# Second-half softmax split in two pieces, its sums and weights placed in the third group of weighting steps; inverse pieces and loads placed anew

## The chip, the cores and the metric

The kernel runs on one NeuronCore of a Trainium2 chip. The time is device microseconds of one execution, from start to end on that core; lower is better. Five engines work side by side, each through its own list of instructions in order: TensorE (PE in the profile, its weight loads PEld), VectorE (DVE), ScalarE (ACT), GpSimd (POOL) and SyncE (SP). SP and POOL also issue the transfers (DMA) of this part of the kernel. An engine waits at an instruction until the semaphores it needs are up, and everything behind that instruction in its list waits too.

## The reference

Two independent operators share one launch; the outputs stand side by side in the last axis. S = L = 2048 positions, D = 640.

```python
# A: 32 heads of 20; each position looks at W=8 positions back, 2 apart
qkv = (x @ wqkv)...                       # q, k, v: [32 heads, 2048, 20]
logits = einsum("bhsd,bhswd->bhsw", q, kg) * 20**-0.5    # kg[s,w] = k[s - 2w]
attn = softmax(where(mask, logits, -1e9))                # over the 8 offsets w
o = einsum("bhsw,bhswd->bhsd", attn, vg)                 # vg[s,w] = v[s - 2w]
a = o.reshape(S, D) @ wo
# B: a diagonal state space kernel K[640, 2048], and the causal convolution with it
K = einsum("dn,dnl,dn->dl", Cc, exp(logdA * l), dB).real
y = irfft(rfft(pad(K)) * rfft(pad(u)))[:2048] + u * Dskip
return concatenate([a, y], axis=-1)
```

## The kernel before

Part B comes first and runs until about 340 us: tables of exponentials and sines, the kernel K by matmuls, and Fourier transforms as matmuls, one chunk c of 128 channels after the other (five chunks). Of its inverse transform the first half ends in DRAM (`Zdram`), and the product of u and the skip factor in `UDdram`. Part A's projections and logits run between and after it. The change is in the last stage, from about 352 us, where three kinds of work share the engines.

**Weighting steps.** `av_step(i0, ni, j0, nj, w)` handles one of the eight offsets w for ni positions of each of four sequence quarters and nj of the five blocks of four head channels. VectorE multiplies v, shifted by 2w, with the weight `at[:, w]` (line 585, tile `prod` or `atp`: a ring of six buffers, two of which are parts of the tile `atp`), then sixteen 32x32 matmuls with the identity add the product into two accumulators `ps_o` of TensorE. After w = 7 ScalarE writes both accumulators to `o` (line 595). So a step's product can't be written before TensorE has read the one six steps earlier. There are six groups of eight steps. By the numbers that the code gives (first position, positions, first block, blocks): the first is (0, 256, 0, 2), then (0, 128, 2, 3), (128, 128, 2, 3), (256, 128, 0, 4), (256, 256, 4, 1) and (384, 128, 0, 4). The first three belong to the first half of the positions (`at[0]`), the last three to the second half (`at[1]`). Three `ps_o` accumulators exist, two of which a group holds, so the second matmul half of a new group waits until ScalarE has emptied the old group's first accumulator.

**Output projection.** `out_proj(q)` makes eight pieces for positions quarter q, each of five 128x128 matmuls with 320 columns (`ps_op<-wo,o`), one evacuation (line 611 on ScalarE, or 609 on VectorE for half of the last eight) and for every second piece a write to the output. The list `rest` holds these pieces. Quarter 0 needs `o` of the first two groups, quarter 1 the third, quarter 2 the fourth and fifth, quarter 3 the sixth.

**Second half of the inverse transform.** 24 pieces in the list `parts` (three for each eight rows, of 3, 3 and 2 rows), each of 12 or 8 matmuls (`ps_ib<-Z,HB`) and one evacuation (line 653) to `ysb`; after each third piece four writes to the output (line 656, on SP). Six pieces use one of four loads `Z` (line 640: fifteen transfers of 128 KB, five chunks of three). The loads 0 and 1 are issued at once; of the loads 2 and 3 single chunks are issued between weighting steps (`LOADS`). Loads 1 and 2 go through SP alone, 0 and 3 through SP and POOL. Pieces of `rest` and `parts` share the two one-bank accumulators.

**Softmax.** `softmax_a(hf)` takes the maximum over the eight offsets (a tree of three operations, line 542), subtracts it, and ScalarE takes the exponential (line 548). `softmax_b(hf)` adds up (a tree of three, line 552), takes the reciprocal (line 557) and writes the weights `at[hf]` (line 561).

From `att.in_order()` on, the matmuls stand in TensorE's list in the order in which the Python code issues them (all recorded at line 420). Instructions of the other engines are put in an order by the planner, unless `keep_in_program_order` holds them. Before the change the planner set VectorE's order: it put weighting step 0 ahead of the last two products of the logits (line 521), and the five operations of `softmax_b(1)` between weighting steps of the first and second group. The code that places it all:

```python
    for w in range(W):                                   # first group
        if w < 2:   fill(parts, 3 - w)
        elif w > 4: fill(parts)
        ...
        att.av_step(0, 256, 0, 2, w)
        if w == 2:   att.softmax_a(1)
        elif w == 4: att.softmax_b(1)
```

In the other five groups a step is followed by a piece of `parts` (second group, odd w; fifth group, each w), by a piece of `rest` (third, fourth and sixth group, each w), and in the sixth group at even w by a piece of `parts` as well.

Of the kernel before, what the change touches and what calls it, by code (L numbers as in the profile page):

```python
# [402 lines left out]
class Attention:  # L403
# [146 lines left out]
    def softmax_b(self, hf):  # L550
        nc, lsb = self.nc, self.lsb[hf]
        TT = lambda o, a, b, op: nc.vector.tensor_tensor(out=o, in0=a, in1=b, op=op)
        tr = self.ta.tile([128, 4, 256], f32, name="tree", tag="TA0")
        TT(tr[:], lsb[:, 0:4], lsb[:, 4:8], A.add)
        TT(tr[:, 0:2], tr[:, 0:2], tr[:, 2:4], A.add)
        TT(tr[:, 0], tr[:, 0], tr[:, 1], A.add)
        nc.vector.reciprocal(out=tr[:, 1], in_=tr[:, 0])
        if hf == 0:
            self.AP_ = self.ta.tile([128, 4, 2048], bf16, name="atp", tag="R1")
        self.at[hf] = self.AP_[:, hf].rearrange("p (w i) -> p w i", w=W)  # L560
        TT(self.at[hf], lsb, tr[:, 1].unsqueeze(1).to_broadcast([128, W, 256]), A.mult)

    def open_out(self, a2):
        nc = self.nc
        self.o = a2.tile([128, 5, S], bf16, name="o")
        self.o4 = self.o[:].rearrange("p j (s i) -> p j s i", s=4)
        self.wo = self.ta.tile([128, 5, D], bf16, name="wo", tag="TX")
        wsrc = self.A_wo.rearrange("(h j dd) e -> dd h j e", j=5, dd=4)
        for dd in range(4):
            nc.gpsimd.dma_start(out=self.wo[32 * dd:32 * dd + 32], in_=wsrc[dd])  # L570
        self.ob = self.ta.tile([128, 6, D], bf16, name="ob", tag="cT")
        ring = self.ta.tile([128, 4, 2048], bf16, name="prod2", tag="R0")
        self.ring = [self.AP_[:, 2], self.AP_[:, 3]] + [ring[:, i] for i in range(4)]

    def av_step(self, i0, ni, j0, nj, w):

        nc = self.nc
        MM = self.MM
        at, n = self.at[i0 // 256], nj * ni
        if w == 0:  # L580
            self.ops = [self.big("ps_o") for _ in range(2)]
        p2 = self.ring[self.nav % 6][:, 0:4 * n]
        self.nav += 1
        off = HALO + i0 - DIL * w
        nc.vector.tensor_tensor(out=p2.rearrange("p (d i) -> p d i", i=ni), in0=self.v2[:, 4 * j0:4 * j0 + 4 * nj, off:off + ni],  # L585
                                in1=at[:, w, i0 % 256:i0 % 256 + ni].unsqueeze(1).to_broadcast([128, 4 * nj, ni]), op=A.mult)
        p2v = p2.rearrange("p (j dd i) -> p dd j i", dd=4, i=ni)
        for sc in range(4):
            for dd in range(4):
                sl = slice(32 * sc, 32 * sc + 32)  # L590
                MM(self.ops[sc // 2][32 * dd:32 * dd + 32, sc % 2, 0:n].rearrange("p (j i) -> p j i", i=ni), lhsT=self.ident[sl, sl], rhs=p2v[sl, dd],
                   start=(w == 0), stop=(w == W - 1), tile_position=(32 * sc, 32 * dd), skip_group_check=True)
        if w == W - 1:
            for f, p in enumerate(self.ops):
                nc.scalar.copy(out=self.o4[:, j0:j0 + nj, 2 * f:2 * f + 2, i0:i0 + ni], in_=p[:, :, 0:n].rearrange("p s (j i) -> p j s i", i=ni))  # L595
# [66 lines left out]
def body(tc, ctx, pools, prm, B_u, B_Dskip, Sd, Zd, UDd, A_x, A_wqkv, A_wo, out_a, out_b):  # L662
    nc = tc.nc
# [33 lines left out]
    att = Attention(tc, pools, A_x, A_wqkv, A_wo, out_a, psk, psg)  # L697
# [86 lines left out]
    a2 = ctx.enter_context(tc.tile_pool(name="a2", bufs=1, side="right", reuse_waits="tile"))  # L784
# [20 lines left out]
    parts = inv.parts()  # L805
    rest = []

    def fill(some, n=1):
        for f in some[0:n]:
            f()  # L810
        del some[0:n]

    for w in range(W):
        if w < 2:
            fill(parts, 3 - w)
        elif w > 4:
            fill(parts)
        if w == 0:
            att.open_out(a2)
        att.av_step(0, 256, 0, 2, w)  # L820
        if w == 2:
            att.softmax_a(1)
        elif w == 4:
            att.softmax_b(1)
    LOADS = {(d, w + 2 * (qr == 3)): (qr, c) for c, (d, w) in enumerate(((0, 0), (0, 4), (1, 0), (1, 4), (None, 0))) for qr in (2, 3)}
    for i0, ni, j0, nj, done in ((0, 128, 2, 3, 0), (128, 128, 2, 3, 1), (256, 128, 0, 4, None), (256, 256, 4, 1, 2), (384, 128, 0, 4, 3)):
        for w in range(W):
            att.av_step(i0, ni, j0, nj, w)
            if (done, w) in LOADS:
                qr, c = LOADS[done, w]  # L830
                inv.load(qr, c, c + 1)
            if done == 2 or done == 0 and w % 2 == 1:
                fill(parts)
            elif done == 0:
                pass
            else:
                fill(rest)
                if done == 3 and w % 2 == 0:
                    fill(parts)
        if done is not None:  # L840
            rest += att.out_proj(done, done == 3)
    for f in parts + rest:
# [4 lines left out]
def kernel(  # L847
# [61 lines left out]
```

## Time and profile before

| | before |
|---|---|
| median of three runs | 439.84 us (439.48 to 441.04) |
| the profiled execution, its own time | 438.98 us |
| span of its trace, first to last instruction | 437.2 us |
| VectorE busy over the span | 391.3 us (89%) |
| TensorE busy over the span | 358.4 us (82%) |
| ScalarE busy over the span | 314.0 us (72%) |
| mean granted TensorE clock | 0.916 |

The profile comes from one execution. Engines' busy times overlap, so shares of the span add up to more than one. A timeline row gives start, duration, engine, line, operation, tiles (written <- read), shapes and how many instructions are merged in the row; in square brackets stands how long the engine sat idle before, and what ended the wait. Durations of neighbouring instructions of one engine overlap a little, so what a piece costs in a dense stretch is the distance from start to start. A row of the windows view gives, for a stretch of time, the busy time (and instructions) of each engine, then the granted clock as a share of full speed, the busy share of the DMA engines and GB/s.

### The profile page before, as it was taken

The numbers are of one execution on the slowest core, as the hardware profiler recorded it, in microseconds if no ns is written. First come the engines' busy times: TensorE is split into PE (matmuls) and PEld (weight loads), VectorE is DVE, ScalarE is ACT, GpSimd is POOL, SyncE is SP. The second block draws the span as 40 slices with busy tenths as digits, with TensorE's granted clock in tenths as the row PEclk, the third lists the DMA queues.
The fourth block names the chain that finished last, engine by engine and source line by source line (L and its number), as shares of the span: only waits on it lengthen the run. The fifth ranks groups of instructions, "written<-read, shape, count | busy, mean of one in ns | idle before, by whom it ended". The sixth has DMA issues, their size and how long they took to land.

```text
span 437.2 us, 17687 instructions
## 1 busy us (share of the span) xinstructions
PE 358.4 (82%) x8041; PEld 241.1 (55%) x8041; DVE 391.3 (89%) x386; ACT 314.0 (72%) x570; POOL 44.5 (10%) x85
## 2 busy tenths in 40 slices
PE   1397659989886998879778799999899897399995
PEld 0145546866863677556665665545555674134443
DVE  7889999999997999999999989946978989999751
ACT  3974998889999899979997845342858344544663
POOL 7440000000000000000010000400001204102110
PEclk9996577999999898889999899999999999659999
DMA  5569102163233402324079933500210907957343
GB/s 143 186 141 200 18 3 109 39 227 94 99 123 123 97 28 98 144 103 99 27 258 241 236 75 135 178 0 3 67 32 1 265 17 201 228 141 225 96 107 114
DMA packets 45131, 51.62 MB, mean 118 GB/s; under 512 B 31376, under 2 KB 38992, under 8 KB 42368
## 3 DMA queue, kind: packets, MB, share of 16 engines
q1 hardware_dynamic: 41520, 41.41, 35.4%
q0 software_dynamic: 3392, 8.95, 7.0%
q8 instruction: 63, 1.03, 1.0%
q10 hardware_dynamic: 144, 0.12, 0.1%
q14 instruction: 12, 0.10, 0.1%
HBM read 28.03 MB, written 18.35 MB: 106 GB/s over the span
## 4 chain that ended last, share of the span: by engine, by line
PE 49%; ACT 29%; DVE 14%; issue 5%; DMA 1%; SPq 1%; DVEq 0%; ACTq 0%
ACT R L222 10%; ACT A L338 6%; PE ps_k L318 6%; PE ps_ph L247 6%; PE ps_k L323 6%; PE ps_op L420 6%; PE ps_k L470 4%; PE ps_q L488 4%; PE ps_ph L250 4%; ACT Sg L344 4%; PE ps_f L343 4%; PE ps_v L501 2%; DVE prod L521 2%; ACT Z L375 2%; PE ps_o L420 2%
## 5 line engine op out<-in xcount | busy, mean ns | idle before, releaser
L305 DVE TENSOR_TENSOR Y<-F,G 128x3072 bf16<-128x3072 bf16 x60 | 102.9, 1751 | 0.6 <-PE ps_k L323 0.6
L222 ACT ACTIVATE R<-LPC 128x192 bf16<-128x192 f32 x225 | 59.3, 358 | 0.1
L247 PE MATMUL ps_ph<-LPC 128*128 128x256 bf16 (+1 forms) x200 | 41.5, 311 | 17.3 <-DMA LPC<-lo 8.7
L318 PE MATMUL ps_k<-Y,X 128*32 128x64 bf16 x1920 | 47.2, 239 | 7.3 <-DVE Y L305 3.8
L323 PE MATMUL ps_k<-Y,X 64*32 64x64 bf16 x1920 | 43.8, 233 | 3.4 <-issue 3.3
L344 ACT CAST Sg<-ps_f 128x1024 bf16<-128x1024 f32 x40 | 37.6, 1027 | 7.3 <-PE ps_f L343 7.3
L318 PEld LDWEIGHTS <-X 128*32 128x32 bf16 x1920 | 32.1, 117 | 17.4 <-issue 9.0
L343 PE MATMUL ps_f<-A,T 128*128 128x128 bf16 x320 | 27.3, 259 | 14.9 <-ACT A L338 14.2
L338 ACT CAST A<-ps_f 128x1024 bf16<-128x1024 f32 x40 | 37.6, 1036 | 0.7 <-PE ps_f L337 0.6
L271 DVE TENSOR_TENSOR X<-R,TX 128x1536 bf16<-128x1536 bf16 x40 | 36.4, 951 | 0.0
L323 PEld LDWEIGHTS <-X 64*32 64x32 bf16 x1920 | 29.6, 113 | 12.1 <-issue 4.4
L255 ACT ACTIVATE TX<-ps_ph 128x864 bf16<-128x864 int16 (+1 forms) x40 | 31.9, 867 | 5.3 <-DVE X L271 2.5
L343 PEld LDWEIGHTS <-T 128*128 128x128 bf16 x320 | 25.6, 119 | 16.1 <-issue 14.9
L585 DVE TENSOR_TENSOR prod<-v,atp 128x2048 bf16<-128x2048 bf16 (+2 forms) x32 | 31.3, 1018 | 2.0 <-PE ps_o L420 1.8
L255 ACT ACTIVATE TA<-ps_ph 128x768 bf16<-128x768 int16 x40 | 30.6, 822 | 3.4 <-PE ps_ph L250 3.0
L250 PE MATMUL ps_ph<-LPC 128*64 128x128 bf16 (+1 forms) x400 | 29.6, 249 | 0.0
L247 PEld LDWEIGHTS <-LPC 128*128 128x128 bf16 x200 | 15.0, 102 | 25.9 <-issue 19.1
L420 PE MATMUL ps_op<-wo,o 128*128 128x320 bf16 x160 | 28.5, 315 | 0.8 <-ACT o L595 0.4
L358 DVE TENSOR_TENSOR P<-P,Sg 128x4096 bf16<-128x4096 bf16 x10 | 22.9, 2288 | 4.1 <-DMA P<-Sdram 3.2
L250 PEld LDWEIGHTS <-LPC 128*64 128x64 bf16 x400 | 15.2, 118 | 19.1 <-issue 18.9
L611 ACT CAST ob<-ps_op 128x320 bf16<-128x320 f32 x28 | 11.9, 431 | 19.0 <-PE ps_op L420 17.3
L337 PE MATMUL ps_f<-BD,U 128*64 128x128 bf16 x320 | 19.4, 285 | 6.1 <-ACT A L338 3.3
(129 smaller groups left out, 661.2 us busy)
## 6 DMA issues: line engine op xcount, KB each, us to landing
Sdram<-Sg SPq DMA_DIRECT2D x5, 1024.0 KB
P<-Sdram SPq DMA_DIRECT2D x5, 1024.0 KB
P<-Sdram SPq DMA_DIRECT2D x10, 512.0 KB
Zdram<-Z SPq DMA_DIRECT2D x5, 1024.0 KB
Z<-Zdram SPq DMA_DIRECT2D x30, 128.0 KB
U<-in_B_u_dram SPq DMA_DIRECT2D x4, 640.0 KB
UDdram<-UD SPq DMA_DIRECT2D x10, 256.0 KB
out_dram<-ysb SPq DMA_DIRECT2D x32, 80.0 KB
```

What stands on the lines that cost most here:

```text
L222: nc.scalar.activation(out=R[:, :, e, :], in_=src, func=ACT.Exp, scale=m)
L247: MM(o[:, :, 0:32], lhsT=L[:, 0:128], rhs=rhs, start=first, stop=last, skip_group_check=True)
L250: MM(o[64 * hh:64 * hh + 64, :, 32:48], lhsT=L[:, 128:192], rhs=rhs[:, :, 16 * hh:16 * hh + 16], start=False, stop=last, skip_group_check= ...
L255: last = nc.scalar.activation(out=dst[:, qs, e0:e0 + 2 * n, :].rearrange("p q (b e) f -> p b e q f", b=2), in_=words.rearrange("p b (e q f ...
L271: TT = lambda o, a, b, op: V.tensor_tensor(out=o, in0=a, in1=b, op=op)
L305: nc.vector.tensor_tensor(out=Y[:].rearrange("p q (b a) f -> p q b a f", a=8), in0=fa, in1=gb, op=A.mult)
L318: MM(ps[32 * g:32 * g + 32, t], lhsT=X[:, q, 2 - k, :, f], rhs=Ys[k][:, q, :, f], start=(t == 0 and k == 0), stop=False, tile_position=(0, ...
L323: MM(ps[32 * g:32 * g + 32, t], lhsT=X[hb, q, 2 - k, :, f], rhs=Ys[k][hb, q, :, f], start=False, stop=(k == 2), tile_position=(64 * (g // ...
L338: nc.scalar.copy(out=A1[:, :, 32 * b:32 * b + 32].rearrange("p k (j g) -> p k j g", g=4), in_=ps[:].rearrange("p j k g -> p k j g"))
L343: last = MM(ps[:, kk], lhsT=C["T2"][:, 8 * b + kk, :], rhs=A1[:, 8 * b + kk, :], start=(kk % 4 == 0), stop=True, skip_group_check=True)
L344: nc.scalar.copy(out=Sg[:, :, 8 * b:8 * b + 8, :], in_=ps[:].rearrange("p k (j g) -> p j k g", g=4))
L420: self.MM = lambda *a, **k: self.tc.keep_in_program_order(self.nc.tensor.matmul(*a, **k))
```

## The change

The first group becomes one of six in a single loop. `softmax_a(1)` stays after step 2 of the first group; `softmax_b(1)` moves from step 4 of the first group to step 3 of the third. Its first operation and all weighting products are held in program order, so that on VectorE the maximum and subtraction stand together after step 2 of the first group, the five operations of sums and weights stand together after step 3 of the third, and step 0 comes behind the last two logit products. Pieces of `parts` per group go from 8, 4, 0, 0, 8, 4 to 6, 6, 4, 0, 8, 0. The eight pieces of the first quarter's output projection, one per step of the third group before, come at steps 0, 1 and 2, and five behind step 3. The loads 2 and 3 are no longer interleaved: one chunk at every second step from step 4 of the first group on, first all of load 2, then load 3. The load of `wo` is issued after step 7 of the first group (`open_wo`).

```diff
-        TT(tr[:], lsb[:, 0:4], lsb[:, 4:8], A.add)
+        first = TT(tr[:], lsb[:, 0:4], lsb[:, 4:8], A.add)
+        if hf == 1:
+            self.tc.keep_in_program_order(first)
...
-        self.wo = self.ta.tile([128, 5, D], bf16, name="wo", tag="TX")
-        wsrc = self.A_wo.rearrange("(h j dd) e -> dd h j e", j=5, dd=4)
-        for dd in range(4):
-            nc.gpsimd.dma_start(out=self.wo[32 * dd:32 * dd + 32], in_=wsrc[dd])
...
+    def open_wo(self):
+        self.wo = self.ta.tile([128, 5, D], bf16, name="wo", tag="TX")
+        wsrc = self.A_wo.rearrange("(h j dd) e -> dd h j e", j=5, dd=4)
+        for dd in range(4):
+            self.nc.gpsimd.dma_start(out=self.wo[32 * dd:32 * dd + 32], in_=wsrc[dd])
...
-        nc.vector.tensor_tensor(out=p2...
+        ins = nc.vector.tensor_tensor(out=p2...
+        self.tc.keep_in_program_order(ins)
...
-    LOADS = {(d, w + 2 * (qr == 3)): (qr, c) for c, (d, w) in enumerate(((0, 0), (0, 4), (1, 0), (1, 4), (None, 0))) for qr in (2, 3)}
...
+    att.open_out(a2)
+    GROUPS = ((0, 256, 0, 2, None), (0, 128, 2, 3, 0), (128, 128, 2, 3, 1), (256, 128, 0, 4, None), (256, 256, 4, 1, 2), (384, 128, 0, 4, 3))
+    LOADS = {4 + 2 * n: (2 + n // NCH, n % NCH) for n in range(2 * NCH)}
+    for group, (i0, ni, j0, nj, done) in enumerate(GROUPS):
         for w in range(W):
+            if group == 0:
+                fill(parts, (2, 1, 1, 2, 0, 0, 0, 0)[w])
             att.av_step(i0, ni, j0, nj, w)
+            if 8 * group + w in LOADS:
+                qr, c = LOADS[8 * group + w]
                 inv.load(qr, c, c + 1)
+            if group == 0:
+                if w == 2:
+                    att.softmax_a(1)
+                elif w == 7:
+                    att.open_wo()
+            elif group == 1:
+                if w > 1:
+                    fill(parts)
+            elif group == 2:
+                if w < 3:
+                    fill(rest)
+                elif w == 3:
+                    att.softmax_b(1)
+                    fill(rest, 5)
+                else:
+                    fill(parts)
+            elif group == 4:
                 fill(parts)
             else:
                 fill(rest)
-                if done == 3 and w % 2 == 0:
-                    fill(parts)
```

More of the change, by code (lines that the diff above doesn't have):

```diff
@@ L566, in open_out @@
         self.o4 = self.o[:].rearrange("p j (s i) -> p j s i", s=4)
+        self.ob = self.ta.tile([128, 6, D], bf16, name="ob", tag="cT")
+        ring = self.ta.tile([128, 4, 2048], bf16, name="prod2", tag="R0")
+        self.ring = [self.AP_[:, 2], self.AP_[:, 3]] + [ring[:, i] for i in range(4)]
+    def open_wo(self):
         self.wo = self.ta.tile([128, 5, D], bf16, name="wo", tag="TX")
@@ L569, in open_out @@
         for dd in range(4):
-            nc.gpsimd.dma_start(out=self.wo[32 * dd:32 * dd + 32], in_=wsrc[dd])
-        self.ob = self.ta.tile([128, 6, D], bf16, name="ob", tag="cT")
-        ring = self.ta.tile([128, 4, 2048], bf16, name="prod2", tag="R0")
-        self.ring = [self.AP_[:, 2], self.AP_[:, 3]] + [ring[:, i] for i in range(4)]
+            self.nc.gpsimd.dma_start(out=self.wo[32 * dd:32 * dd + 32], in_=wsrc[dd])
     def av_step(self, i0, ni, j0, nj, w):
@@ L584, in av_step @@
         off = HALO + i0 - DIL * w
-        nc.vector.tensor_tensor(out=p2.rearrange("p (d i) -> p d i", i=ni), in0=self.v2[:, 4 * j0:4 * j0 + 4 * nj, off:off + ni],
+        ins = nc.vector.tensor_tensor(out=p2.rearrange("p (d i) -> p d i", i=ni), in0=self.v2[:, 4 * j0:4 * j0 + 4 * nj, off:off + ni],
                                 in1=at[:, w, i0 % 256:i0 % 256 + ni].unsqueeze(1).to_broadcast([128, 4 * nj, ni]), op=A.mult)
+        self.tc.keep_in_program_order(ins)
         p2v = p2.rearrange("p (j dd i) -> p dd j i", dd=4, i=ni)
@@ L811, in fill @@
         del some[0:n]
[L813 to L816, printed above, removed]
-            fill(parts)
[L818 to L824, printed above, removed]
-    LOADS = {(d, w + 2 * (qr == 3)): (qr, c) for c, (d, w) in enumerate(((0, 0), (0, 4), (1, 0), (1, 4), (None, 0))) for qr in (2, 3)}
-    for i0, ni, j0, nj, done in ((0, 128, 2, 3, 0), (128, 128, 2, 3, 1), (256, 128, 0, 4, None), (256, 256, 4, 1, 2), (384, 128, 0, 4, 3)):
+    att.open_out(a2)
+    GROUPS = ((0, 256, 0, 2, None), (0, 128, 2, 3, 0), (128, 128, 2, 3, 1), (256, 128, 0, 4, None), (256, 256, 4, 1, 2), (384, 128, 0, 4, 3))
+    LOADS = {4 + 2 * n: (2 + n // NCH, n % NCH) for n in range(2 * NCH)}
+    for group, (i0, ni, j0, nj, done) in enumerate(GROUPS):
         for w in range(W):
+            if group == 0:
+                fill(parts, (2, 1, 1, 2, 0, 0, 0, 0)[w])
             att.av_step(i0, ni, j0, nj, w)
-            if (done, w) in LOADS:
-                qr, c = LOADS[done, w]
+            if 8 * group + w in LOADS:
+                qr, c = LOADS[8 * group + w]
                 inv.load(qr, c, c + 1)
-            if done == 2 or done == 0 and w % 2 == 1:
+            if group == 0:
[15 more added lines that the diff above has]
+            elif group == 4:
                 fill(parts)
-            elif done == 0:
-                pass
             else:
                 fill(rest)
-                if done == 3 and w % 2 == 0:
-                    fill(parts)
         if done is not None:
```

## The prediction

> **What bounds the kernel now.** I read first the windows view over the last stage, cut where a group's work ends on TensorE, because the shares of the whole span mix stages.
>
> ```profile
> core 0: us, PE busy (x) PEld busy (x) DVE busy (x) ACT busy (x) POOL busy (x), PEclk, DMA share, GB/s
> 361.20:387.70 26.50, 16.04 (x476) 7.83 (x468) 25.53 (x25) 12.12 (x19) 6.13 (x11) 0.74 0.79 193
> 387.70:409.60 21.90, 21.86 (x368) 9.68 (x368) 19.90 (x22) 10.14 (x21) 3.83 (x7) 0.84 0.63 187
> 409.60:426.70 17.10, 15.97 (x425) 7.82 (x424) 10.62 (x11) 11.58 (x25) 2.16 (x4) 1.00 0.39 100
> ```
>
> Up to 387.7 VectorE is busy 25.53 of 26.50 us and TensorE 16.04, at a mean clock of 0.74. From then on TensorE has no gap (21.86 of 21.90 us) while VectorE begins to wait. The timeline says how far TensorE is behind:
>
> ```profile
> 403.52 1.52 DVE L585 TENSOR_TENSOR prod<-v,atp 128x1024 bf16<-128x1024 bf16 x2
> 405.50 0.69 DVE L585 TENSOR_TENSOR prod<-v,atp 128x1024 bf16<-128x1024 bf16 x1 [0.46 <-PE ps_o L420]
> 408.77 0.85 PE L420 MATMUL ps_op<-wo,o 128*128 128x320 bf16 x5
> 420.04 0.32 PE ps_ib L420 x12
> 425.84 0.84 PE L420 MATMUL ps_op<-wo,o 128*128 128x320 bf16 x5
> ```
>
> VectorE starts the fifth group at 403.52 and is soon held by the ring (0.46 us until TensorE's `ps_o`); TensorE ends its last piece of the fourth group at 409.62, 6 us later. From there it needs 17.06 us to the end of the sixth group (426.68), and a tail follows that the change doesn't touch. The fourth row is from the chain of waits: a `parts` piece, 0.32 us on the path, one of four that stand in the sixth group. So TensorE's backlog sets the end, and the reader should ask where it comes from.
>
> ```profile
> 378.81 0.59 PE L420 MATMUL ps_ib<-Z,HB 96*32 96x160 bf16 x12 [3.81 <-DMA Z<-UDdram]
> 384.15 0.55 PE L420 MATMUL ps_o<-prod,ident 32*32 32x384 bf16 x16 [0.25 <-DVE prod L585]
> 385.15 0.55 PE L420 MATMUL ps_o<-atp,ident 32*32 32x384 bf16 x16
> 391.43 1.51 PE L420 MATMUL ps_op<-wo,o 128*128 128x320 bf16 x5
> 392.88 0.54 PE L420 MATMUL ps_o<-atp,ident 32*32 32x384 bf16 x16
> 393.35 1.42 PE L420 MATMUL ps_op<-wo,o 128*128 128x320 bf16 x5
> 396.90 0.38 PE L420 MATMUL ps_o<-prod,ident 32*32 32x384 bf16 x16
> 397.21 0.85 PE L420 MATMUL ps_op<-wo,o 128*128 128x320 bf16 x5
> 402.65 0.43 PE L420 MATMUL ps_o<-prod,ident 32*32 32x512 bf16 x16
> 403.02 0.85 PE L420 MATMUL ps_op<-wo,o 128*128 128x320 bf16 x5
> 403.80 0.43 PE L420 MATMUL ps_o<-prod,ident 32*32 32x512 bf16 x16
> ```
>
> First cause: at 378.81 TensorE had waited 3.81 us for load 1 of the inverse. Second: it then runs slowly. Step plus `parts` piece takes 1.00 us (384.15 to 385.15), step plus projection piece 1.92 (391.43 to 393.35), the piece alone 1.45; later the same pair takes 1.15 (402.65 to 403.80), the projection piece 0.78, a 384-column step 0.31 (396.90 to 397.21). The granted clock says why:
>
> ```profile
> 114.66:118.07 3.41, 1.78 (x32) 1.73 (x31) 3.41 (x4) 3.41 (x7) 0.62 (x2) 1.00 0.71 291
> 118.07:121.48 3.41, 3.41 (x33) 2.87 (x32) 3.41 (x4) 3.41 (x5) 0.00 (x0) 0.50 0.02 5
> 370.66:374.07 3.41, 0.34 (x25) 0.17 (x8) 2.51 (x3) 2.49 (x3) 1.12 (x3) 1.00 1.04 222
> 374.07:377.48 3.41, 0.94 (x24) 0.19 (x23) 3.41 (x5) 0.76 (x2) 0.53 (x1) 0.50 1.09 246
> 387.72:391.14 3.42, 3.38 (x61) 1.16 (x60) 3.42 (x5) 1.91 (x4) 0.00 (x0) 0.50 0.70 209
> 391.14:394.55 3.41, 3.41 (x42) 1.29 (x26) 3.41 (x5) 0.77 (x2) 0.57 (x1) 0.50 0.57 132
> 394.55:397.96 3.41, 3.41 (x65) 1.63 (x63) 3.41 (x4) 1.27 (x3) 0.56 (x1) 1.00 0.82 250
> ```
>
> After 0.34 us of work in 370.66 to 374.07 the clock is 0.50, and it stays there up to 394.55, through a stretch with 3.38 of 3.42 us busy; only after a stretch filled with projection pieces (391.14 to 394.55) is it 1.00.
>
> **VectorE's chain after the change.** The diff of the orders gives: two logit products, step 0, steps 1 and 2, maximum and subtraction, steps 3 to 7, second group, four steps, sums and weights in one block, four steps, and the rest as before.
>
> ```profile
> 363.88 0.61 ACT L535 ACTIVATE lsb<-ps_l 128x512 f32<-128x512 f32 x1
> 362.34 3.49 DVE L585 TENSOR_TENSOR prod<-v,atp 128x2048 bf16<-128x2048 bf16 x3
> 368.02 1.15 DVE L542 TENSOR_TENSOR tree<-tree 128x512 f32<-128x512 f32 x2
> 369.20 2.29 DVE L542 TENSOR_TENSOR lsb<-lsb,tree 128x2048 f32<-128x2048 f32 x1
> 371.58 1.91 ACT L548 ACTIVATE lsb<-lsb 128x2048 f32<-128x2048 f32 x1 [2.19 <-DVE lsb L542]
> 373.53 1.23 DVE L552 TENSOR_TENSOR tree<-lsb 128x1024 f32<-128x1024 f32 x1 [0.90 <-ACT lsb L548]
> 378.48 1.75 DVE L557 RECIPROCAL tree<-tree 128x256 f32<-128x256 f32 x1
> 380.95 2.28 DVE L552 TENSOR_TENSOR atp<-lsb,tree 128x2048 bf16<-128x2048 f32 x1
> 385.75 3.56 DVE L585 TENSOR_TENSOR prod<-v,atp 128x1536 bf16<-128x1536 bf16 x4
> 388.21 1.50 ACT L595 CAST o<-ps_o 128x768 bf16<-128x768 f32 x2 [0.64 <-PE ps_o L420]
> ```
>
> Step 0 behind the logit products costs nothing: it fills a wait that step 1 has anyway for v's halo, so step 2 still starts at 362.34. Three steps of 2048 elements in 3.49 us make 1.14 a step, four of 1536 in 3.56 make 0.87. Step 2 ends at 363.5; the maximum needs the last logits, which ScalarE ends at 364.49: 1.0 us of idle, in place of the 0.90 us before 373.53 that VectorE now waits for the exponential. Maximum and subtraction 1.23 + 1.15 + 2.29 end at 369.2; five steps of 1.14 end the first group at 374.9, eight of 0.87 the second at 381.9, four more 385.4. The block is 1.23 + 1.15 (two tree operations as above) + 1.75 + 2.28 = 6.4 us: up to 391.8, some 0.45 more than when steps stood between, since no neighbours overlap. Four steps to 395.3, eight of 1.14 to 404.4. That is 0.9 later than 403.52, hidden as long as TensorE is further behind than that.
>
> **TensorE after the change.** First group: six pieces in place of eight, none of which needs load 1. Pieces 2 to 5 wait for evacuations that stand behind the exponential (1.91 us, now from about 369.2) in ScalarE's order: up to 371.5, no step of the ring is late by that. Step 2 of the second group is written at 377.6, and the first piece that needs load 1 stands behind it. That load waits for the last logit product on VectorE, which now ends one step (1.14) earlier, so it lands between 377.7 and the 378.81 of before; I take 378.8. The cover of TensorE's work for this load is gone, but the wait shrinks from 3.81 to about 1.
>
> I take the clock to fall again around 377.5: in 370.7 to 377.5 TensorE has only a step of about 0.4 us in 0.87 to 1.14, and a stretch with 1.78 of 3.41 us busy was followed by 0.50 (114.66, above). Then, at half clock: five pairs of 1.00 from 378.8, the last step done at 383.8. ScalarE empties both accumulators in 1.50: 385.4. A projection piece 1.45, two pairs of 1.92, a step 0.47: 391.2. Here stands what the change makes of VectorE's block: five projection pieces, with no step to wait for. The stretch from 387.7 to 391.1 is now as full of them as 391.14 to 394.55 was, so full clock from 391.1: five of 0.78, 395.1. Four steps with `parts` pieces, (0.31 + 0.32) each, 397.7; VectorE had them ready at 395.3. Fourth group: 8 x 1.15 and 0.4 for the accumulators at the boundary (half of the 1.50, less a piece), 407.3 against 409.62.
>
> From there 17.06 us less the four pieces that left the sixth group, 4 x 0.32 = 1.28: the end of the sixth group at 423.1, against 426.68. **The sum: -3.6 us**, of which 2.3 come from work moved ahead into TensorE's idle and half-clock time, and 1.3 from the shorter last group. Bounds: one clock stretch of 3.41 us more or less at half clock moves it by 3.41 x (1.45 - 0.78) / 1.45 = 1.6.
>
> **Loads and queues.** `wo` keeps its place in POOL's queue, behind load 0 and ahead of POOL's share of load 3; nothing moves there. On SP the fifteen transfers of load 2 now stand together behind eight output writes, ahead of the writes of pieces 6 to 11, and SP's eight of load 3 go behind.
>
> ```profile
> 359.43 1.88 SPq L640 DMA_DIRECT2D Z<-Zdram  x2
> 379.46 1.36 SPq L640 DMA_DIRECT2D Z<-Zdram  x2
> 397.71 3.29 SPq L640 DMA_DIRECT2D Z<-Zdram  x3
> ```
>
> The first of load 2 goes out at 379.46 as before (a write ahead of it waits for load 1). Two issues take 1.36 us, three in the worst row 3.29: fifteen end at 389.7 to 396. The first piece of load 2 is due at 395.4. The high end is the fifteen of load 1, 359.43 to 378.81, 19.4 us in all, amid the loads of `wo`: that would land at 398.9. I take 392, near the two-issue row, since those other loads are over by then, and so no cost. Output writes held behind load 2 are done long before a buffer of `ysb` is needed again.
>
> **Rivals.**
> (1) *The clock doesn't fall, or is back a stretch early.* TensorE then ends the third group behind VectorE's 395.3, at 396, and both need 1.15 a step: 405.7, sixth group's end 421.5, a gain of 5.2. For it: there is no gap as long as that of 370.66 to 374.07. Against it: the 114.66 row. The Trainium skill (TensorE: Matmul & The Clock Gate, Part 1) has it that the clock halves after an idle window of about 3.4 us and is whole again after one busy window; by that rule the clock stays up here and this rival comes true. The trace agrees on the idle stretch at 370.66, but not on 114.66 (half busy, yet followed by 0.50) nor on 387.72 (busy 3.38 of 3.42, and still 0.50 after it).
> (2) *Load 2 is late.* If it lands at 398.9, the first piece of load 2 is held from 395.4 on, 3.5 us, with every step behind it: the gain is gone. For it: all fifteen transfers have to be there for the first piece, in place of being spread over the steps up to 397.71 and later. Against: the issue rows.
> (3) *Slower: the block freezes the half clock.* VectorE's 6.4 us without steps leave TensorE with five projection pieces and then steps at 0.87 apart; if that doesn't bring the clock back, each us at half clock costs 0.45, and 3.6 / 0.45 = 8 us beyond 391.1 eat the gain: it decides from 399. Half clock up to 401.4, three stretches more, is 1.0 us slower; through the whole fourth group (8 x 1.92 for 8 x 1.15, with 3.3 for the pieces and 1.5 for the steps ahead) 7.4 slower. For it: 20.5 us at half clock in the trace. Against: one stretch full of projection pieces ended them.
>
> **How the numbers follow.** The profiled execution took 438.98 us for its span of 437.2; three runs have a median of 439.84, and their lowest is 0.5 above the profiled one. I set the sum against 438.98 and add 0.4, half the distance to the median. Forecast, chance 0.52: 438.98 + 0.4 - 3.6 = 435.8 (its own range 434.2 to 437.4). Rival 1, 0.22: 434.2. Rival 2, 0.15: 439.4. Rival 3, 0.11: 440.4 to 446.8. The range 433.6 to 439.3 holds the first two and most of the third. Half a per cent, 2.2 us, is what a measurement of this kernel can tell from no change; faster by more means under 437.6: forecast and rival 1, 0.74; within, rival 2, 0.15; slower, rival 3, 0.11.
>
> **What would show it.** VectorE: a wait of about 1 us ahead of the maximum, none for the exponential, a 6.4 us block from about 385.4, the fifth group's start near 404.4. TensorE: a wait for load 1 under 1.5 us; half clock ending by 391 or so; the fourth group's last piece near 407; no `ps_ib` in the sixth group, and its end near 423. I am wrong if TensorE waits for load 2 at the third group's step 4, if the half clock lasts beyond 399, or if the fourth group's end on TensorE hasn't moved.

## The result, and the profile after

| | before | changed |
|---|---|---|
| median, 19 runs each, taken in turns | 441.43 us (438.24 to 446.03) | 438.51 us (434.11 to 443.71) |
| ratio to before, 95% interval | | 0.9928 [0.9899, 0.9958] |
| the profiled execution, its own time | 438.98 us | 434.11 us |
| span of its trace | 437.2 us | 432.3 us |
| mean granted TensorE clock | 0.916 | 0.937 |

The ratios here and below leave out, for both kernels, the runs more than 1.5% above their kernel's fastest: four of the changed kernel's 19, and three of the six of the later kernel mix, its profiled one among them. The ratio means 3.2 us less. The profiled execution is the fastest of the changed kernel's 19, and 4.9 us below that of before: the median must lose some of it in a way that this trace doesn't show. That is what the experiments had to find.

The windows view of the changed kernel, cut at TensorE's start of the first projection piece and its ends of the fourth and the sixth group, and then four single stretches of the clock:

```profile
core 0: us, PE busy (x) PEld busy (x) DVE busy (x) ACT busy (x) POOL busy (x), PEclk, DMA share, GB/s
361.20:385.86 24.66, 19.73 (x504) 8.88 (x497) 23.49 (x24) 13.36 (x22) 6.14 (x11) 0.71 0.84 215
385.86:406.38 20.52, 20.21 (x380) 10.16 (x373) 20.38 (x21) 10.97 (x24) 3.84 (x7) 0.94 0.69 200
406.38:421.89 15.51, 14.42 (x381) 6.99 (x380) 11.98 (x13) 9.91 (x21) 2.17 (x4) 1.00 0.42 109
368.04:371.46 3.42, 1.91 (x80) 0.91 (x69) 3.42 (x3) 3.02 (x4) 3.04 (x6) 1.00 0.94 233
385.11:388.52 3.41, 3.35 (x40) 1.27 (x32) 3.31 (x5) 1.70 (x4) 0.00 (x0) 0.50 0.67 196
388.52:391.94 3.42, 3.42 (x52) 1.97 (x51) 3.39 (x3) 1.33 (x4) 0.58 (x2) 1.00 0.61 190
405.59:409.00 3.41, 2.62 (x84) 1.40 (x85) 3.41 (x7) 3.16 (x6) 0.54 (x1) 1.00 0.15 53
```

The same cut in the kernel before, whose first projection piece begins at 389.51:

```profile
361.20:389.51 28.31, 17.81 (x500) 8.29 (x493) 27.34 (x27) 13.42 (x21) 6.13 (x11) 0.73 0.78 194
```

About the same 500 matmuls now lie ahead of that piece, in 24.66 us in place of 28.31, since VectorE has no block to do there (23.49 us of work in place of 27.34). From then to the fourth group's end neither engine has a gap (20.21 and 20.38 of 20.52 us): they run side by side. The clock falls after the stretch from 368.04 and is back after that from 385.11: 17.1 us at half, in place of 20.5.

VectorE's timeline in the changed kernel:

```profile
364.63 1.23 DVE L542 TENSOR_TENSOR tree<-lsb 128x1024 f32<-128x1024 f32 x1 [0.97 <-ACT lsb L535]
369.29 3.48 DVE L589 TENSOR_TENSOR prod<-v,atp 128x2048 bf16<-128x2048 bf16 x3
385.39 1.22 DVE L552 TENSOR_TENSOR tree<-lsb 128x1024 f32<-128x1024 f32 x1
389.61 2.29 DVE L552 TENSOR_TENSOR atp<-lsb,tree 128x2048 bf16<-128x2048 f32 x1
391.82 3.56 DVE L589 TENSOR_TENSOR prod<-v,atp 128x1536 bf16<-128x1536 bf16 x4
404.38 2.49 DVE L589 TENSOR_TENSOR prod<-v,atp 128x1024 bf16<-128x1024 bf16 x4
```

One wait of 0.97 us for the last logits ahead of the maximum, none for the exponential, and the block from 385.39 to 391.82. TensorE's timeline, from the first piece that needs load 1:

```profile
376.85 1.40 PE L420 MATMUL ps_o<-prod,ident 32*32 32x384 bf16 x40 [0.37 <-ACT o L600]
378.29 0.59 PE L420 MATMUL ps_ib<-Z,HB 96*32 96x160 bf16 x12
380.16 0.51 PE L420 MATMUL ps_o<-prod,ident 32*32 32x384 bf16 x5 [0.82 <-issue]
385.86 1.51 PE L420 MATMUL ps_op<-wo,o 128*128 128x320 bf16 x5
390.32 3.57 PE L420 MATMUL ps_op<-wo,o 128*128 128x320 bf16 x25
394.27 0.39 PE L420 MATMUL ps_ib<-Z,HB 96*32 96x160 bf16 x12
405.53 0.85 PE L420 MATMUL ps_op<-wo,o 128*128 128x320 bf16 x5
421.04 0.85 PE L420 MATMUL ps_op<-wo,o 128*128 128x320 bf16 x5
```

At 378.29 there is no wait for the load (the 40 matmuls ahead end at 378.25). The five projection pieces of VectorE's block are the row at 390.32. The fourth group's last piece ends at 406.38, 2.0 us after VectorE's start of the fifth group (404.38); before it was 6. The sixth group's last piece ends at 421.89 (before 426.68). SP's queue has the first and last transfers of load 2 here:

```profile
379.02 1.19 SPq L645 DMA_DIRECT2D Z<-Zdram  x2
...
389.06 0.59 SPq L645 DMA_DIRECT2D Z<-UDdram  x1
```

The piece that needs load 2 is the one at 394.27, and it waits for nothing.

### The profile page after: what moved, and what is told of

Same layout as the page of the kernel before. It is cut to its first block, busy times and chain, and to the rows that moved or that the text cites. A ratio compares the mean times of both kernels' runs of the same rounds, so it can differ in the third digit from the quotient of the medians.

```text
span 432.3 us, 17695 instructions
## 1 busy us (share of the span) xinstructions
PE 361.1 (84%) x8041; PEld 243.0 (56%) x8041; DVE 391.2 (90%) x386; ACT 314.3 (73%) x570; POOL 44.4 (10%) x85
## 4 chain that ended last, share of the span: by engine, by line
PE 47%; ACT 27%; issue 10%; DVE 9%; DMA 4%; POOL 1%; SPq 1%; DVEq 0%; ACTq 0%; POOLq 0%
ACT R L222 10%; ACT A L338 7%; PE ps_k L318 6%; PE ps_ph L247 6%; PE ps_k L323 6%; PE ps_ph L250 4%; PE ps_f L343 4%; PE ps_k L470 4%; PE ps_q L488 4%; PE ps_v L501 4%; ACT Sg L344 3%; PE ps_op L420 3%; DVE prod L521 2%; ACT Z L375 2%; DVE X L271 2%
## 5 line engine op out<-in xcount | busy, mean ns | idle before, releaser
L222 ACT ACTIVATE R<-LPC 128x192 bf16<-128x192 f32 x225 | 59.3, 359 | 0.1
L247 PE MATMUL ps_ph<-LPC 128*128 128x256 bf16 (+1 forms) x200 | 42.4, 316 | 15.8 <-DMA LPC<-lo 8.2
L343 PEld LDWEIGHTS <-T 128*128 128x128 bf16 x320 | 25.3, 118 | 16.1 <-issue 14.9
L247 PEld LDWEIGHTS <-LPC 128*128 128x128 bf16 x200 | 15.2, 104 | 24.6 <-issue 9.5
L420 PE MATMUL ps_op<-wo,o 128*128 128x320 bf16 x160 | 26.9, 308 | 0.7 <-ACT ob L616 0.4
```

Of the source, the lines that this page charges most:

```text
L222: nc.scalar.activation(out=R[:, :, e, :], in_=src, func=ACT.Exp, scale=m)
L247: MM(o[:, :, 0:32], lhsT=L[:, 0:128], rhs=rhs, start=first, stop=last, skip_group_check=True)
L343: last = MM(ps[:, kk], lhsT=C["T2"][:, 8 * b + kk, :], rhs=A1[:, 8 * b + kk, :], start=(kk % 4 == 0), stop=True, skip_group_check=True)
L420: self.MM = lambda *a, **k: self.tc.keep_in_program_order(self.nc.tensor.matmul(*a, **k))
```

## The experiments

All ran beside runs of the kernel before, in three batches (35, 29 and 27 runs of it; a "call" in the expectations below is such a batch). The span of a single profile is a poor measure here: ScalarE's last evacuation of logits (line 535 in both), ahead of everything that the change touches, ended at 364.5 us in the first profile of the kernel before and at 369.4 in a second one of the very same kernel. So the table measures the *stage*: from the end of that evacuation to the end of the sixth group's last projection piece (in the changed kernel 364.60 and 421.89: 57.3 us). "Fourth" is the end of the fourth group's last step on TensorE, "rest" what lies between that and the stage's end, and "half clock" the lengths of the spells at half clock between the stage's start and its end. The ratio is to the kernel before of the same batch. Each kernel has one profile a batch, so a stage is one execution.

| kernel | batch | median us | ratio [95%] | stage | fourth | rest | half clock |
|---|---|---|---|---|---|---|---|
| before, first profile | | | | 62.2 | 44.3 | 17.9 | 20.5 |
| before2 | 3 | 440.35 | 1.0011 [0.9975, 1.0048] | 62.0 | 44.2 | 17.7 | 20.5 |
| changed, first profile | | 438.51 | 0.9928 [0.9899, 0.9958] | 57.3 | 41.0 | 16.3 | 17.1 |
| again | 1 | 438.45 | 0.9953 [0.9921, 0.9985] | 60.9 | 42.2 | 18.6 | 20.5 and 6.8 |
| again2 | 3 | 440.02 | 1.001 [0.9978, 1.0042] | 61.5 | 42.9 | 18.6 | 20.5 and 6.8 |
| block_first | 1 | 442.78 | 1.0053 [1.0018, 1.0088] | 66.5 | 46.5 | 20.0 | 23.9 and 10.2 |
| parts_only | 1 | 441.42 | 0.9968 [0.993, 1.0007] | 60.7 | 44.4 | 16.3 | 20.5 |
| parts_last | 1 | 439.19 | 0.995 [0.9914, 0.9986] | 59.3 | 41.4 | 17.8 | 20.5 |
| rest_spread | 2 | 438.14 | 0.9963 [0.9924, 1.0002] | 61.4 | 42.9 | 18.5 | 20.5 and 6.8 |
| loads_mixed | 3 | 445.49 | 1.0125 [1.0077, 1.0172] | 68.3 | 52.2 | 16.1 | 20.5 and 13.7 |
| warm | 2 | 437.17 | 0.9898 [0.9854, 0.9943] | 57.5 | 41.2 | 16.3 | none |
| warm_mix | 2 | 436.07 | 0.9913 [0.9876, 0.9949] | 57.2 | 40.3 | 16.9 | 3.4 |
| mix | 2 | 437.90 | 0.9876 [0.9808, 0.9945] | 58.1 | 41.2 | 16.9 | 20.5 |
| mix2 | 3 | 435.52 | 0.9905 [0.9862, 0.9947] | 57.9 | 41.0 | 16.9 | 20.5 |

**The changed kernel once more (again, again2), and the kernel before (before2).** No edit; these are the yardsticks of their batches.

> The changed kernel once more, for a second profile. The stage is counted from the end of the last logits' evacuation on ScalarE (364.49 us before, 364.60 after) to the end of the sixth group's last projection piece on TensorE (426.68, 421.89): 62.2 us before, 57.3 after. If the gain is a property of the order, the stage is 57 to 59 again, whatever the span is, and a longer span has its extra time ahead of 364 us. If the profiled run was lucky with the clock, half clock lasts a stretch longer here and the stage is 58.5 to 60.

> The changed kernel a third time. Two profiles gave stages of 57.3 us (half clock once) and 60.9 (a second spell from 47 us after the logits). If the spell is a matter of where the clock's stretches fall on the fifth group, either may come; the stage is within 57 to 58.5 or within 60 to 61.5 us and nothing between that the half clock of the first spell doesn't explain.

> The kernel before, for a second profile of it: 62.2 us again if no second spell comes; with one of 6.8 us in the fifth group some 3.4 us more, 65 to 66. If a second profile without a spell gave 58 to 60 us, the gain seen in the first pair of profiles would be chance.

The gain was 0.5% in the first batch and nothing that can be told in the third. Against the first profile of the changed kernel, again's stage is 3.6 us longer, beyond both ranges expected of it: about 1.2 up to the fourth group's end, where the half clock lasts one stretch longer, and 2.3 behind it. Windows of again2, two of the first spell and three of the fifth and sixth group, show what happens:

```profile
387.36:390.77 3.41, 3.35 (x53) 1.10 (x45) 3.31 (x5) 2.30 (x4) 0.00 (x0) 0.50 0.61 184
390.77:394.18 3.41, 3.41 (x42) 1.44 (x42) 3.38 (x2) 0.85 (x2) 0.57 (x1) 0.50 0.59 179
411.25:414.66 3.41, 2.71 (x124) 1.51 (x123) 2.86 (x4) 2.82 (x6) 0.54 (x1) 1.00 0.24 72
414.66:418.08 3.42, 3.42 (x104) 1.36 (x96) 3.42 (x4) 2.61 (x7) 0.00 (x0) 0.50 0.48 103
418.08:421.49 3.41, 3.41 (x34) 1.29 (x26) 3.41 (x4) 0.88 (x3) 0.00 (x0) 0.50 0.71 155
```

After the stretch from 411.25, in which TensorE is busy 2.71 of 3.41 us, the clock is at half for two stretches, in the middle of the fifth group. A second spell, that neither profile of the kernel before has. The first profile of the changed kernel had no more work than that in a stretch of its fifth group (2.62 us from 405.59) and kept its clock.

**The block where it was (block_first).** The first group issues the sums and weights again, everything else as changed.

```diff
                 if w == 2:
                     att.softmax_a(1)
+                elif w == 4:
+                    att.softmax_b(1)
...
                 elif w == 3:
-                    att.softmax_b(1)
                     fill(rest, 5)
```

> The block of sums and weights goes back to step 4 of the first group; pieces, loads and the held order stay as in the changed kernel. My theory: the place of the block is what counts, since it lets the second group end 6.4 us earlier on VectorE and the projection pieces with it; without it TensorE meets them at about 391 in place of 385.9 and the stage is 61 to 63 us (57.3 with the block late), the time about that of before. Rival: the gain comes from the pieces of the inverse moved ahead and the shorter sixth group; then the stage stays at 57 to 58.5.

Half a per cent slower than the kernel before, and the stage longer than the 61 to 63 us expected. First VectorE's, then TensorE's timeline of this kernel:

```profile
370.67 1.22 DVE L552 TENSOR_TENSOR tree<-lsb 128x1024 f32<-128x1024 f32 x1
...
374.90 2.29 DVE L552 TENSOR_TENSOR atp<-lsb,tree 128x2048 bf16<-128x2048 f32 x1
```

```profile
378.38 0.66 PE L420 MATMUL ps_o<-prod,ident 32*32 32x512 bf16 x16 [3.66 <-DVE prod L589]
...
389.99 1.51 PE L420 MATMUL ps_op<-wo,o 128*128 128x320 bf16 x5
```

The block now stands at 370.67 to 377.19, while TensorE has nothing else to do: it waits 3.66 us for the next product, and its first projection piece begins 26.3 us after the logits' end, in place of 21.3. Of the 5.6 us that the stage is longer than again's, 4.2 are there at the fourth group's end already; the other 1.4 go with a second spell of 10.2 us. With the other edits kept, one block in the first group is worse than the five operations between steps that the kernel before has there; a block is good only where TensorE has other work to go on with.

**The pieces and loads alone (parts_only).** The kernel before, with the pieces of `parts` (6, 6, 4, 0, 8, 0 per group) and the loads as in the changed kernel, and the softmax where the planner put it.

```diff
-        if w < 2:
-            fill(parts, 3 - w)
-        elif w > 4:
-            fill(parts)
+        fill(parts, (2, 1, 1, 2, 0, 0, 0, 0)[w])
...
-            if done == 2 or done == 0 and w % 2 == 1:
+            if done == 2 or done == 0 and w > 1:
                 fill(parts)
...
                 fill(rest)
-                if done == 3 and w % 2 == 0:
+                if done == 1 and w > 3:
                     fill(parts)
```

> The kernel before with the changed placing of inverse pieces (6, 6, 4, 0, 8, 0) and of loads 2 and 3, the softmax and VectorE's order left to the planner. My theory: the stage is 60.5 to 62.5 us, since the 1.3 us taken out of the sixth group come back in the third, where TensorE is behind; ratio to before 0.995 to 1.003. Rival (the pieces are the gain): 57 to 58.5 us and 0.990 to 0.994.

Between the two: its fourth group ends where before's does (44.4 against 44.3), and the rest takes 16.3 in place of 17.9. So taking four pieces out of the sixth group gives 1.6 by itself, and gives it also without the block. What is gained up to the fourth group (1.4 to 3.3 us in the three profiles of the changed kernel) is missing here, with the softmax and VectorE's order as before; it is missing too in block_first, which keeps the held order and moves only the block. So it needs the block's place. TensorE's timeline of this kernel has the wait that remains:

```profile
372.96 0.92 PE L420 MATMUL ps_ib<-Z,HB 96*32 96x160 bf16 x20 [3.85 <-ACT ysb L653]
```

An evacuation of `ysb` stands behind the exponential on ScalarE, and TensorE's list can't go past it: 3.85 us, in the changed kernel 1.65.

**Four pieces back in the sixth group (parts_last).**

```diff
                     fill(rest, 5)
-                else:
-                    fill(parts)
...
                 fill(rest)
+                if done == 3 and w % 2 == 0:
+                    fill(parts)
```

> The changed kernel with four inverse pieces back in the sixth group (6, 6, 0, 0, 8, 4). My theory: in the third group they fill time that TensorE has free behind the block, so taking them out gains nothing there, and the sixth group gets 4 x 0.32 = 1.3 us longer: stage 58.3 to 59.3 us. Rival (pieces are most of the gain): 61 us or more. Rival (they are hidden anyway): 57 to 57.6.

Two of the four in TensorE's timeline of this kernel:

```profile
416.86 0.32 PE L420 MATMUL ps_ib<-Z,HB 96*32 96x160 bf16 x8
...
419.41 0.39 PE L420 MATMUL ps_ib<-Z,HB 96*32 96x160 bf16 x12
```

Its rest is 17.8 against 16.3 in the changed kernel's profile without a second spell, 1.5 more, about what before has over parts_only (17.9 against 16.3). The median can't tell this kernel from again.

**The five pieces spread (rest_spread).** One projection piece at each step of the third group, and VectorE's block as in the changed kernel.

```diff
-                if w < 3:
-                    fill(rest)
-                elif w == 3:
-                    att.softmax_b(1)
-                    fill(rest, 5)
-                else:
-                    fill(parts)
+                fill(rest)
+                if w == 3:
+                    att.softmax_b(1)
+                elif w > 3:
+                    fill(parts)
```

> The changed kernel with one projection piece behind every step of the third group, in place of five behind step 3: TensorE has one piece, not five, to do in the 6.4 us in which VectorE adds up the second half's weights. Theory: the four others come back behind steps 4 to 7, where a step with both pieces takes 0.31 + 0.32 + 0.78 against VectorE's 0.87; 4 x 0.78 less what TensorE has to spare there, 2 to 3 us more at the third group's end, and a longer half clock besides: stage 59 to 62 us. Rival (TensorE has room, VectorE sets the end anyway): 57 to 58 us.

The stage is 61.4, and its fourth group ends at 42.9; again and again2, with the same two spells, have 60.9 and 61.5, and 42.2 and 42.9. So filling VectorE's block on TensorE is worth 0.6 us at most, and by the ratios nothing that can be told. TensorE's backlog at that point is long enough to go on with, whatever it works on.

**The loads in turns (loads_mixed).** Chunks of the loads 2 and 3 take turns, as before the change.

```diff
-    LOADS = {4 + 2 * n: (2 + n // NCH, n % NCH) for n in range(2 * NCH)}
+    LOADS = {4 + 2 * n: (2 + n % 2, n // 2) for n in range(2 * NCH)}
```

> The changed kernel with the chunks of loads 2 and 3 issued alternately, as before the change, at the changed steps. The last chunk of load 2 then stands on SP behind all of load 3 and behind twelve output writes, the last four of which wait for the second group's last piece. Theory (load 2 ahead is needed for pieces in the third group): TensorE waits for load 2 at the third group's step 4, at about 394.6, for 2 to 5 us, and the stage is 59 to 62 us. Rival (the placing of loads is free): no wait for Z in the third group, stage 57 to 58 us, or 60 to 61 with a second spell in the fifth group.

SP's queue and then TensorE's timeline of this kernel:

```profile
399.98 1.83 SPq L645 DMA_DIRECT2D Z<-Zdram  x3
401.85 0.60 SPq L645 DMA_DIRECT2D Z<-UDdram  x1
402.50 0.54 SPq L645 DMA_DIRECT2D Z<-Zdram  x1
403.08 0.59 SPq L645 DMA_DIRECT2D Z<-UDdram  x1
```

```profile
406.18 0.59 PE L420 MATMUL ps_ib<-Z,HB 96*32 96x160 bf16 x12 [5.99 <-DMA Z<-Zdram]
```

TensorE waits 5.99 us at the third group's step 4 for load 2, whose transfers now go out until 403.7, and a spell of 13.7 us at half clock begins in the wait. Both the wait and the stage are longer than expected (2 to 5 us, 59 to 62). The second rival's mechanism is real; what keeps it out of the changed kernel is that load 2 goes ahead of load 3.

**A busy TensorE (warm).** Behind some steps of the first two groups, matmuls with a tile of zeros are added into the same accumulators, one to five a step: nothing of the result changes, TensorE is merely kept at work.

```diff
+        for i in range(idle):
+            MM(self.ops[i % 2][:, 0, 0:n], lhsT=self.zero[:], rhs=self.v2[:, 0, 0:n], start=False, stop=False, skip_group_check=True)
...
+    IDLE = {2: 5, 3: 2, 4: 2, 5: 2, 6: 2, 8: 2, 9: 2, 10: 1, 11: 1, 12: 1, 13: 1, 14: 1}
...
-            att.av_step(i0, ni, j0, nj, w)
+            att.av_step(i0, ni, j0, nj, w, IDLE.get(8 * group + w, 0))
```

> The changed kernel with matmuls that add zeros to the accumulators, where TensorE is idle in the first and second group (five behind step 2, two behind each of steps 3 to 6 and of the second group's steps 0 and 1, one behind each of its steps 2 to 6). Theory: half clock from 371 to 388 comes from TensorE's light load there; with the zeros it stays whole, the third group's first projection piece comes 1 us earlier or not at all, and the stage is 56 to 57.5 us where no second spell follows (VectorE sets the pace there), 59.5 to 60.5 where one does. Rival: the clock falls all the same, and the zeros run at half speed: stage 58 to 62 us.

Windows of this kernel, from the first steps to the fourth group's end:

```profile
361.90:386.00 24.10, 19.77 (x495) 9.17 (x487) 22.92 (x23) 11.80 (x20) 6.13 (x11) 1.00 0.84 211
386.00:406.51 20.51, 19.47 (x397) 9.90 (x392) 20.37 (x21) 11.81 (x25) 3.83 (x7) 1.00 0.71 203
```

The clock is 1.00 in both, and in the rest of the stage. Yet the stage takes 57.5 us, no less than the changed kernel's best (57.3, with 17.1 us at half clock), and its fourth group ends no sooner (41.2 against 41.0). From 386 on VectorE is busy 20.37 of 20.51 us: it sets the pace now. So a first spell of 17.1 us costs the changed kernel nothing that these two profiles show, and full clock in its place has nothing to give. One of 20.5 us does cost something: up to the fourth group's end again and again2 take 1.0 and 1.7 us longer than warm.

**Heavier work in the fifth group (mix, mix2, warm_mix).** Two projection pieces of the fourth group change places with two `parts` pieces of the fifth. mix2 is mix in another batch, beside again2; warm_mix is warm and mix together.

```diff
+            elif group == 3:
+                fill(parts if w in (3, 6) else rest)
             elif group == 4:
-                fill(parts)
+                fill(rest if w in (1, 4) else parts)
```

> The changed kernel with two of the eight projection pieces of the fourth group exchanged for inverse pieces of the fifth (inverse pieces at steps 3 and 6 of the fourth group, projection pieces at steps 1 and 4 of the fifth): the same work, no stretch of the fifth group without a full-array matmul. Theory: the second spell at half clock that the second profile of the changed kernel shows in the fifth and sixth group (6.8 us, stage 60.9 against 57.3 us) comes from the light work of the fifth group; here it is gone, the stage is 56.8 to 58 us in each profile and the ratio to before 0.988 to 0.993, below that of the changed kernel. Rival: the spell comes by chance of the clock's own state, whatever the load; then the ratio is that of the changed kernel (0.993 to 0.995).

> The exchange of two pieces between the fourth and the fifth group once more. Theory: no second spell, stage 56.8 to 58.3 us; ratio to before 0.988 to 0.993 and under that of the changed kernel in the same call. Rival: ratios of both the same, 0.992 to 0.996.

> Both of these edits. Theory: no spell at half clock between the logits and the tail; stage 56 to 57.5 us, ratio to before 0.985 to 0.992. Rival: as the changed kernel, 0.993 to 0.995.

A window of mix2 in the fifth group, and two steps of TensorE's timeline there:

```profile
408.04:411.45 3.41, 3.27 (x105) 1.90 (x106) 3.41 (x6) 2.50 (x6) 0.54 (x1) 1.00 0.47 121
```

```profile
408.77 0.85 PE L420 MATMUL ps_op<-wo,o 128*128 128x320 bf16 x5
...
410.90 0.85 PE L420 MATMUL ps_op<-wo,o 128*128 128x320 bf16 x5
```

The stretch that begins 0.91 us behind the fifth group's first step is now busy 3.27 of 3.41 us, and neither profile of this kernel has a second spell. In the third batch it stands at 0.9905 [0.9862, 0.9947], where the changed kernel beside it stands at 1.001 [0.9978, 1.0042]: it beats both kernels. Its medians are 437.90 and 435.52. The lower ratio of mix rests on three runs; its median of six is 0.993 of the 440.94 before beside it. warm_mix gains nothing more.

## Why the prediction was right, and where it wasn't

**VectorE's chain.** Every time of it came within 0.1 us: the wait ahead of the maximum 0.97 (about 1), the steps from 369.29 (369.2), the block 385.39 to 391.82 (385.4 to 391.8), the third group's end 395.3, the fifth group's start 404.38 (404.4). Distances from start to start in the trace of before were enough for it.

**Load 1.** About 1 us of wait was forecast, and none came (378.29). A step later TensorE is idle for 0.82 us for no reason that the profile shows ("issue"), in again2 for 1.9; so the first projection piece is at 385.86 against 385.4 all the same.

**The half clock.** Its fall was put at 377.5, and it came at 371.46, after a stretch in which TensorE was busy 1.91 of 3.42 us: the row from 114.66 that the prediction quoted (1.78 of 3.41, then 0.50) applied two stretches earlier than I applied it. That cost little, since the steps up to 378 come at VectorE's pace of 1.14 us. Its end was put 26.6 us after the logits' end; it was 26.5 and 27.0 in again and again2, and 23.9 in the first profile, one stretch earlier. So the first profile went the way of the first rival from there (fourth group's end 406.38, sixth's 421.89; the rival had 405.7 and 421.5, and 434.2 us against the 434.11 of that execution, which is a coincidence in part: the rival's time was for a median, and this execution is the fastest of 19), and the others the way of the forecast (fourth group's last step 42.2 and 42.9 us after the logits' end; the forecast's 407.3, less 364.49 and the 0.78 of the piece behind that step, is 42.0).

**What brings the clock back.** In the first profile of the changed kernel the clock came back after the stretch from 385.11, busy 3.35 of 3.41 us; in again2 it didn't after the stretch from 387.36, busy 3.35 of 3.41 us too. The Trainium skill (TensorE: Matmul & The Clock Gate, Part 1) has one busy window bring the full clock back and an idle one of about 3.4 us take it away. The first pair speaks against the one half, and again2's fall after 2.71 us of work from 411.25 against the other. The last section has a count of work that tells these stretches apart.

**Block, pieces, load 2.** That the block's place and TensorE's work moved ahead give the gain up to the fourth group is shown by block_first and parts_only; the five pieces behind step 3, which the prediction made much of, count for 0.6 us or less (rest_spread). The four pieces out of the sixth group were put at 1.28 and measure 1.5 to 1.6. Load 2 was put at 389.7 to 396 for its last issue; it was 389.65.

**What failed.** The step "From there 17.06 us less the four pieces that left the sixth group" takes it that the fifth and sixth groups run at full clock, as they did before. In the first profile they do (15.51 us from 406.38 to 421.89, forecast 15.8). In again and again2 they don't: their rest is 18.6 in both in place of 16.3, and these 2.3 us are half of the 4.9 that the first profile's stage had gained. Over the three measurements (0.9928, 0.9953 and 1.001) the change gives between 0.7% and nothing. The third rival saw a lasting half clock as the danger, but put it at VectorE's block; it came later, in another group. Hence 438.51 and not 435.8. Of the 2.7 us between, 1.6 are that the kernel before had a median of 441.43 beside it and not 439.84; the other 1.1 are a gain smaller than forecast.

That the second spell costs these 2.3 us is read from profiles of one kernel with and without it. That it is what sets the median is argued: each kernel has one profile a batch, and the runs without a profile show no spells. Their mean granted clock is no help: it is 0.937 in the first profile and 0.901 in again's, and the 10.2 us more at half clock in again's stage make only 0.012 of that. The exchange in mix2, whose profile lacks it and which gains 1% where again2 gains nothing, speaks for it.

## What to carry to other kernels

A gain in a stage with a clock of two states is worth what later groups keep of it: read the clock behind the edit too, and in more than one profile. Here the clock fell in a group of nothing but small matmuls; large ones exchanged into it cost nothing, and in the one batch that had both kernels they were worth more than the change itself. And where executions of one kernel differ by more than an edit gives, measure the edit from the last event ahead of it.

## What the runs showed of the hardware

The clock goes in stretches of 3.41 us whose place against the program differs from one execution to the next. In the 14 profiles the second spell came in the four in which a stretch began between 0.11 us ahead of the fifth group's first step on TensorE and 0.60 us behind it (block_first, rest_spread, again2, again, in this order), so that the whole stretch held only 256-column steps, `parts` pieces and the two waits for evacuations at the group's start. In the other ten the nearest beginning of a stretch was 0.72 us or more ahead of that step, so that the stretch took in projection work (0.72 in the changed kernel's first profile, at 405.59 against 406.31; 1.35 and 1.46 in those of the kernel before), or 0.90 us or more behind it (0.90 and 0.91 in mix and mix2, so that these two profiles can't tell their heavier group from a lucky place; only the ratios speak for it). Before, the same light group was there with like waits, and the stretches lay otherwise. What the chip weighs is left open. The busy share alone it isn't (2.62 of 3.41 us kept the clock, 2.71 lost it), and stretches full of small matmuls (3.42 of 3.42 us busy from 414.66 in again2) didn't bring it back, while one of mostly projection pieces (418.08) did.

One count of work fits the stage much better. Take each matmul's columns times the share of the 128*128 array that its shape names (1/16 for 32*32), in units of one projection matmul (128*128 with 320 columns), and add up what starts in a stretch. Over all stretches of the 14 stages, at full clock none with more than 9.1 was followed by half clock (151 of them), and each with less than 8.0 was (9); between, nine kept the clock and nine lost it. At half clock each with 9.2 or less stayed there (68), and each with 9.8 or more was followed by full clock (18). So the two stretches busy 3.35 us differ: 9.8 from 385.11 in the first profile, 8.2 from 387.36 in again2. In the fifth group it is 9.1 for the stretch that kept the clock in the first profile, 8.1 for the one that lost it in again2, and 15.2 from 408.04 in mix2, which speaks for the heavier group. This was read out of the profiles afterwards: no run varied the count by itself, and it doesn't tell the stretches of earlier parts of the program apart.

Matmuls with zeros count as work: warm has no spell at all in its stage, where every kernel without them has a first one of 17.1 us or more. And TensorE's idle time put down to "issue" in the middle of a step, 0.7 to 1.9 us at a time in the first two groups of most of these kernels, has no cause in the trace.
